# Spectral layer and two expert layers on one core: when constants are loaded, and how weight decoding is spread

## The chip, the core and the metric

The kernel runs on one core of a Trainium2 chip. Times are microseconds of device time for one execution; the kernel before has three of them and their median is what the prediction is compared with. The profile is of one further execution.

## The reference, cut to what matters

```python
X = np.fft.rfft(x, axis=1)                    # x: 2 x 3008 x 256, float32
Yr = Xr @ w_r - Xi @ w_i + b_r
Yi = Xr @ w_i + Xi @ w_r + b_i
Yr, Yi = shrink(Yr, 0.01), shrink(Yi, 0.01)   # soft threshold
y = np.fft.irfft(Y, n=3008, axis=1)
h = y @ w_in;   y = (h - tanh(h)) @ w_out                      # 256 x 2048, 2048 x 256
h = y @ w_in2;  out = (h * clip(h + 3, 0, 6) / 6) @ w_out2     # the same sizes
```

The four expert matrices arrive as float64.

## The kernel before, in words

**First stage: the spectral layer.** 3008 is split as 47 x 64. `dft_a` (16 calls, 8 per batch; L270) transforms along 47 with the matrix `amt`, two PSUM banks per call; ACT copies the banks back into the tile of x (L288) and stores it to DRAM, `s1` (L289). Batch 0 is done ahead of the main loop from eight tiles `xa`, batch 1 inside it from a ring of three tiles `xb`. The main loop (L664) has 24 iterations t, each on two of the 2 x 24 rows. `load_bi` reads `s1` back into a ring of three (`bi_all`, 512 KB for two iterations); a batch's first such load needs all eight of its stores. `dft_b(t+2)` (L310) transforms along 64 with the constants `bmt`; ACT evicts it as high part `fh` (L317, L318), DVE makes the low part `fl` (L324), ACT a negated copy (`evict_b_neg`, L329). `linear(t)` is 24 matmuls with the weights. `shrink(t)` is three DVE instructions (L351 to L353); then ACT makes `sh` and DVE `sl` (`shrink_split`, by L115 and L116). `dft_c(t-2)` transforms back along 64 with `cmH` and `cmL`; ACT evicts it (L377) and SP stores it to `s2`. Each pair of loads of `cmH` and `cmL` (2 x 256 KB, on POOL's queue, L623) serves two iterations. `dft_d` (L403) with `dmt` (35 KB) ends the transform and makes the operands of the second stage.

**Weight decoding.** The 32 blocks ("units") of the four matrices, 1i, 1o, 2i, 2o with 8 each, come as raw float64 words (512 KB a unit, `w_load`, on SP's queue, three buffers) and are made into two float32r parts by a generator, `w_steps`. The loops advance it step by step with `w_step`, so decoding is laid between other work by hand. A unit has seven steps (kind i, with four sums more) or five (kind o): two ACT instructions (L168, L169); two DVE tensor_scalars (L171, L172); the low part of the unit before (L203); a DVE instruction that frees the raw buffer and behind it the next `w_load` (L175); an addition (L179); for kind i four sums (L185 to L189); ACT's rounding to the high part (L197). `ptr["dec"]` counts finished units. In the first stage there are two steps before `shrink_split` and NST = 3 after it, from t = 0 until NDEC = 16 units are done, all of 1i and then all of 1o; the units of the second matrix pair follow in the second stage, and go back to DRAM.

**Second stage: the experts.** Sixteen super-groups k (0 to 7 the first expert, 8 to 15 the second) of eight groups g. A group (`group`, L568) is seven products into the banks al, be and ga in a scheme of sums (Strassen's), the nonlinearity, and the output matmuls of the group before into the four banks `acc`. Group (0,0) is written out as `first_group` at the end of the first stage. `super_hook` is called at five points (a to e) of a group; it lays the decode steps (three per group, at b, c and d: in all groups of k = 0, in groups 1 to 5 of k = 1 to 7) and the preparation of the next operands. `w_until` runs the generator on until a unit is done; it stands only at super-group 7 and after.

**What sets the order.** The kernel is written under a manual schedule: every engine and every DMA queue takes its instructions in program order, with the waits of their tiles. SP's queue carries x, raw, bmt, bi_all and the stores to s2; ACT's the stores to s1; POOL's the loads of cm. PSUM has eight banks: al (2), be, ga, and acc (4); `bank("h")` walks through al, be, al, ga.

Of the kernel before, what the change touches and what calls it, by code (L numbers as in the profile page):

```python
# [87 lines left out]
def spectral_moe_kernel(ctx: ExitStack, tc: tile.TileContext, x, w_r, w_i, b_r, b_i,  # L88
# [35 lines left out]
    wst = ctx.enter_context(tc.tile_pool(name="wst", bufs=2))  # L124
    dmt = perm.tile([96, 94], F32, name="dmt")
    three = perm.tile([128, 1], F32, name="three")
    wia = ctx.enter_context(tc.tile_pool(name="wia", bufs=1))
    wpool, W = {}, {}

# [4 lines left out]
        W[nm, c] = pl.tile([128, 2, n], F32R, tag=f"w{kind}{c}", name=f"w{kind}{c}")  # L134
        return W[nm, c]

    NDEC, NST = 16, 3
    w_src = {"1i": w1i, "1o": w1o, "2i": w2i, "2o": w2o}
    w_order = [(nm, c) for nm in ("1i", "1o", "2i", "2o") for c in range(8)]
    w_raw = {}  # L140
    ptr = {"load": 0, "dec": 0}

    def w_load(n=1):
        for _ in range(n):
            if ptr["load"] >= len(w_order):
# [12 lines left out]
    w_ws = {}  # L158

    def w_words(nm, c):  # L160
        u = w_raw.pop((nm, c)).bitcast(U32).rearrange("p (n two) -> p n two", two=2)
        lw, hw = u[:, :, 0], u[:, :, 1]
        ws = wst.tile([128, 8, 128], F32, tag="ws", name="ws")
        w_ws[nm, c] = ws
        taf = ws[:, 0:4, :].rearrange("p a f -> p (a f)")
        ta = taf.bitcast(U32)
        rnd = ws[:, 4:8, :].rearrange("p a f -> p (a f)").bitcast(U32)
        act.activation(out=taf, in_=hw.bitcast(F32), func=ACTF.Abs)  # L168
        act.activation(out=rnd, in_=lw, func=ACTF.Copy, scale=2.0 ** -29)  # L169
        yield  # L170
        dve.tensor_scalar(out=taf, in0=taf, scalar1=CLAMP, scalar2=None, op0=ALU.max)  # L171
        dve.tensor_scalar(out=ta, in0=ta, scalar1=3, scalar2=0x3FFFFFF8,  # L172
                          op0=ALU.logical_shift_left, op1=ALU.bitwise_and)
        yield "lo"
        dve.scalar_tensor_tensor(out=ta, in0=hw, scalar=0xC0000000, in1=ta,  # L175
                                 op0=ALU.bitwise_and, op1=ALU.bitwise_or)
        w_load()
        yield
        dve.tensor_tensor(out=ta, in0=ta, in1=rnd, op=ALU.add)  # L179

    def w_sums(nm, c):
        ws = w_ws[nm, c]
        if nm[1] == "i":
            yield
            dve.tensor_tensor(out=ws[:, 4, :], in0=ws[:, 0, :], in1=ws[:, 2, :], op=ALU.add)  # L185
            dve.tensor_tensor(out=ws[:, 6, :], in0=ws[:, 1, :], in1=ws[:, 0, :], op=ALU.subtract)
            yield
            dve.tensor_tensor(out=ws[:, 5, :], in0=ws[:, 4, :], in1=ws[:, 1, :], op=ALU.subtract)
            dve.tensor_tensor(out=ws[:, 7, :], in0=ws[:, 3, :], in1=ws[:, 5, :], op=ALU.subtract)  # L189
            src = ws[:, 1:8, :].rearrange("p a f -> p (a f)")  # L190
        else:
            src = ws[:, 0:4, :].rearrange("p a f -> p (a f)")
        if nm[0] == "1":
            t = alloc_w(nm, c)
        else:
            t = mo["w"].tile([128, 2, 896 if nm[1] == "i" else 512], F32R, tag="wout", name="wout")
        act.activation(out=t[:, 0, :], in_=src, func=ACTF.Copy)  # L197
        w_ws[nm, c] = (t, src)
        yield

    def w_lo(nm, c):
        t, src = w_ws.pop((nm, c))
        dve.tensor_tensor(out=t[:, 1, :], in0=src, in1=t.bitcast(F32)[:, 0, :], op=ALU.subtract)  # L203
        if nm[0] == "2":
            sp.dma_start(out=(w2id if nm[1] == "i" else w2od)[c], in_=t.bitcast(F32))

    def w_steps():
        for k, unit in enumerate(w_order):
            for step in w_words(*unit):
                yield  # L210
                if step == "lo" and k:
                    w_lo(*w_order[k - 1])
                    ptr["dec"] = k
                    yield
            yield from w_sums(*unit)
        w_lo(*w_order[-1])
        ptr["dec"] = len(w_order)

    w_gen = w_steps()

# [49 lines left out]
    def dft_a(i, finish=True):  # L270
        b, c = divmod(i, 8)
        xt = (x1[c % 3] if b else x0[c])[0:96]
        banks_ = []
        for g in range(2):
            p = bank("h")
            pv = p[0:96].rearrange("p (u d) -> p u d", d=D)
            for u in range(2):
                pe.matmul(out=pv[:, u, :], lhsT=amt, rhs=xt[:, 2 * g + u, :], start=True, stop=True)
            banks_.append(pv)
        if finish:  # L280
            dft_a_out(i, banks_)
        return banks_
# [71 lines left out]
        s = y  # L354
        s_t[j] = (s, sh, sl)

    def shrink_split(j, eng):
        s, sh, sl = s_t[j]
        split(sh, sl, s, eng)
        s_t[j] = (sh, sl)  # L360

    def dft_c(j):
# [250 lines left out]
    with tc.manual_schedule():  # L613
# [3 lines left out]
            if g < 6:  # L617
                sp.dma_start(out=bmt[:, 4 * g:4 * g + 4, :], in_=bv[:, 4 * g:4 * g + 4, :])

        def load_cm(g):  # L620
            if g < 6:
                for h, t in enumerate((cmH, cmL)):
                    pool.dma_start(out=t[:, 512 * g:512 * g + 512], in_=cm[:, h, 512 * g:512 * g + 512])  # L623

# [19 lines left out]
        load_bi(1)  # L644
        load_x(8)
        load_x(9)
        w_load()
# [16 lines left out]
        for t in range(NP):  # L664
            linear(t)
            if t > 1:
                dft_c(t - 2)
            if t + 2 < NP:
                dft_b(t + 2)
            ab = dft_a(a_next, False) if a_next < 16 else None  # L670
            if t > 1:
                evict_c(t - 2)
            if t + 2 < NP:
                evict_b_hi(t + 2)
            shrink(t)
            if t + 2 < NP:
                evict_b_lo(t + 2)
            if t == NP - 1:
                first = first_group()
                next(first)  # L680
            for _ in range(2):
                if ptr["dec"] < NDEC:
                    w_step()
            shrink_split(t, dve)
            for nm in {20: ("b11", "b21"), 21: ("t1",), 22: ("t2", "b22")}.get(t, ()):
                op_lo(0, nm)
            if t == 20:
                op_sub(T1, B12, B11, dve)
            if t == 21:
                op_sub(T2, B22, T1, dve)  # L690
            if t + 2 < NP:
                evict_b_neg(t + 2)
            if ab:
                dft_a_out(a_next, ab)
                a_next += 1
            flush_stores()
            if t % 2 == 0:
                load_bm(t // 2 + 2)
                load_cm(t // 2 + 1)
            if t > 0:  # L700
                load_x(10 + t)
            if t % 2 == 1:
                load_bi((t + 1) // 2 + 2)
            for _ in range(NST):
                if ptr["dec"] < NDEC:
                    w_step()
            if t == 9:
                sp.dma_start(out=dmt, in_=dm)
            if t == 14:
                load_din(0, din0)  # L710
            if t == 17:
                load_din(1, bi_ring[0])
            if t in (16, 17):
                dft_d(0, t - 16, "h")
            if t in (19, 20):
                dft_d(1, t - 19, "h")
            for nm in {19: ("b11", "b21"), 20: ("t1",), 21: ("t2", "b22")}.get(t, ()):
                op_hi(0, nm)
            if t == 22:
                op_sub(T3, B22, B12)  # L720
                op_sub(T4, B21, T2)
# [15 lines left out]
        def super_hook(k, g, pos):  # L737
# [92 lines left out]
```

## Time and profile before

| | us |
|---|---|
| median of 3 runs | 1255.49 (1254.61 to 1255.74) |
| the profiled execution | 1255.02 |
| its span, first to last instruction | 1253.2 |
| busy: PE, DVE, ACT, POOL | 1196.6, 974.3, 879.2, 165.0 |

The span and the execution's own time differ by what lies around the first and the last instruction. PE is TensorE, DVE VectorE, ACT ScalarE, POOL GpSimd, SP the engine that issues most of the DMAs. L12 is line 12 of the kernel. An instruction row has its start, its length, engine, line, operation, output and input; in brackets stand the idle time ahead of it on its engine and what ended it. The busy shares are means over stages that have different limits, so the rows further on are cut by stage.

### The profile page before, as it was taken

What the parts mean: (1) busy time and instruction counts of PE and PEld (TensorE: products, weight loads), DVE (VectorE), ACT (ScalarE), POOL (GpSimd) and SP (SyncE); (2) the same over time, 40 slices, a digit from 0 to 9 for tenths busy, and PEclk for the clock granted to TensorE, in tenths of its full rate; (3) what the DMA queues carried; (4) which work ended last, traced back from release to release, by engine and by line L of the source; (5) the groups of instructions that cost most, each with busy time, mean ns of one, the idle gap of its engine ahead of it and who ended that gap; (6) DMA issues with size and microseconds to landing.
All of it is one profiled execution on the core that took longest, in us unless ns stands there. A gap on an engine that the chain in (4) does not pass through costs nothing.

```text
span 1253.2 us, 20926 instructions
## 1 busy us (share of the span) xinstructions
PE 1196.6 (95%) x7824; PEld 1167.3 (93%) x7824; DVE 974.3 (78%) x1833; ACT 879.2 (70%) x1836; POOL 165.0 (13%) x165
## 2 busy tenths in 40 slices
PE   6788799989999999999999999999999999999998
PEld 4688698989999999999999999999999999999998
DVE  0487988788888888888868787878787878787775
ACT  3365666777777777777767677777777777777775
POOL 3000000220202020110202130202020202020200
PEclk8889999999999999999999999999999999999999
DMA  9874642131222222202001650000001010101000
GB/s 312 247 232 154 184 152 85 58 115 63 76 68 73 71 76 68 85 26 72 29 1 49 215 195 11 22 30 22 30 14 38 11 40 8 44 5 46 1 26 25
DMA packets 47797, 96.51 MB, mean 77 GB/s; under 512 B 4448, under 2 KB 27488, under 8 KB 47696
## 3 DMA queue, kind: packets, MB, share of 16 engines
q1 hardware_dynamic: 41728, 74.08, 18.8%
q0 software_dynamic: 4032, 14.68, 3.6%
q10 hardware_dynamic: 1936, 6.42, 1.5%
q8 instruction: 61, 1.00, 0.3%
q14 instruction: 40, 0.33, 0.1%
HBM read 58.73 MB, written 36.44 MB: 76 GB/s over the span
## 4 chain that ended last, share of the span: by engine, by line
PE 59%; DVE 17%; ACT 16%; issue 4%; DMA 3%; SPq 0%; ACTq 0%; DVEq 0%
PE acc L119 10%; PE acc L120 10%; PE acc L121 10%; PE al L119 5%; PE al L120 5%; PE al L121 5%; ACT gh L115 5%; DVE g L445 4%; DVE gl L116 3%; PE be L121 2%; PE be L120 2%; PE be L119 2%; ACT e L444 2%; DVE g L448 1%; PE ga L119 1%
## 5 line engine op out<-in xcount | busy, mean ns | idle before, releaser
L116 DVE TENSOR_TENSOR gl<-g,gh 128x376 fp32r<-128x376 f32 x502 | 286.4, 571 | 149.9 <-ACT gh L115 120.1
L115 ACT ACTIVATE gh<-g 128x376 fp32r<-128x376 f32 x509 | 263.9, 518 | 188.0 <-DVE g L445 92.6
L120 PE MATMUL acc<-wo,gh 128*128 128x256 f32 (+1 forms) x768 | 215.7, 281 | 0.0
L119 PE MATMUL acc<-wo,gh 128*128 128x256 f32 (+1 forms) x768 | 215.5, 281 | 0.0
L121 PE MATMUL acc<-wo,gl 128*128 128x256 f32 (+1 forms) x768 | 215.2, 280 | 0.0
L119 PE MATMUL acc<-gh,wo 128*128 128x376 f32 x512 | 173.2, 338 | 0.0
L121 PE MATMUL acc<-gh,wo 128*128 128x376 f32 x512 | 171.0, 334 | 0.0
L120 PE MATMUL acc<-gl,wo 128*128 128x376 f32 x512 | 171.0, 334 | 0.0
L412 POOL TENSOR_TENSOR bmt<-bmt 128x376 f32<-128x376 f32 x62 | 74.9, 1208 | 593.3 <-ACT bmt L405 449.3
L121 PEld LDWEIGHTS acc<-wo,gl 128*128 128x128 f32 (+1 forms) x768 | 143.0, 186 | 0.0
L120 PEld LDWEIGHTS acc<-wo,gh 128*128 128x128 f32 (+1 forms) x768 | 142.9, 186 | 0.0
L119 PEld LDWEIGHTS acc<-wo,gh 128*128 128x128 f32 (+1 forms) x768 | 142.7, 186 | 0.0
L448 DVE SCALAR_TENSOR_TENSOR g<-e,c 128x376 f32<-128x376 f32 x192 | 118.5, 617 | 12.6 <-ACT e L447 8.7
L445 DVE TENSOR_TENSOR g<-c,e 128x376 f32<-128x376 f32 x189 | 113.6, 601 | 14.0 <-ACT e L444 11.8
L447 ACT ACTIVATE e<-c,three 128x376 f32<-128x376 f32 x192 | 117.0, 609 | 7.7 <-DVE c L594 7.3
L428 POOL TENSOR_TENSOR cmL<-bmt,cmH 128x376 fp32r<-128x376 f32 x60 | 64.9, 1082 | 317.8 <-ACT cmH L423 317.8
L444 ACT ACTIVATE e<-c 128x376 f32<-128x376 f32 x189 | 97.8, 517 | 3.9 <-DVE c L594 3.7
L119 PE MATMUL al<-cmH,wi 128*128 128x376 f32 x256 | 88.6, 346 | 9.1 <-ACT s L580 7.4
L119 PEld LDWEIGHTS acc<-gh,wo 128*128 128x128 f32 x512 | 96.4, 188 | 0.0
L120 PEld LDWEIGHTS acc<-gl,wo 128*128 128x128 f32 x512 | 96.2, 188 | 0.0
L121 PEld LDWEIGHTS acc<-gh,wo 128*128 128x128 f32 x512 | 96.2, 188 | 0.0
L584 ACT ACTIVATE s<-be 128x376 f32<-128x376 f32 x127 | 61.9, 487 | 37.7 <-PE be L121 37.7
(164 smaller groups left out, 2870.9 us busy)
## 6 DMA issues: line engine op xcount, KB each, us to landing
raw<-in_moe_w_in_dram SPq DMA_DIRECT2D x16, 512.0 KB, 4.3
raw<-in_moe_w_out_dram SPq DMA_DIRECT2D x16, 512.0 KB, 4.2
w2id<-wout SPq DMA_DIRECT2D x8, 896.0 KB, 3.7
wi<-w2id POOLq DMA_DIRECT2D x8, 896.0 KB, 4.9
bi_all<-s SPq DMA_DIRECT2D x12, 512.0 KB, 4.4
y1d<-y SPq DMA_DIRECT2D x32, 188.0 KB, 2.5
bmt<-y1d SPq DMA_DIRECT2D x8, 752.0 KB, 5.2
s<-co SPq DMA_DIRECT2D x23, 256.0 KB, 2.9
```

The costliest lines, as they stand in the source:

```text
L115: act.activation(out=hi, in_=src, func=ACTF.Copy)
L116: (lo_eng or dve).tensor_tensor(out=lo, in0=src, in1=hi.bitcast(F32), op=ALU.subtract)
L119: pe.matmul(out=out_ap, lhsT=lh, rhs=rh, start=start, stop=False, **kw)
L120: pe.matmul(out=out_ap, lhsT=lh, rhs=rl, start=False, stop=False, **kw)
L121: pe.matmul(out=out_ap, lhsT=ll, rhs=rh, start=False, stop=stop, **kw)
L412: eng.tensor_tensor(out=out, in0=a, in1=b, op=ALU.subtract)
L428: (eng or dve).tensor_tensor(out=l, in0=OPS[nm][0], in1=h.bitcast(F32), op=ALU.subtract)
L444: act.activation(out=e, in_=src, func=ACTF.Tanh)
L445: dve.tensor_tensor(out=g, in0=src, in1=e, op=ALU.subtract)
L447: act.activation(out=e, in_=src, func=ACTF.Relu, bias=three)
L448: dve.scalar_tensor_tensor(out=g, in0=e, scalar=6.0, in1=src, op0=ALU.min, op1=ALU.mult)
L584: act.activation(out=s5, in_=be, func=ACTF.Copy)
```

## The change

Constants: `load_cm` gets a second argument; a one-element copy on POOL that reads it stands ahead of each pair of cm loads. The first pair reads the last tile of batch 0's `dft_a`, the others `sh` of the iteration that issues them. `dmt` is loaded at the start instead of at t = 9; `load_x(8)` stands ahead of `load_bi(0)`, `load_x(9)` ahead of `load_bi(1)`. Of the three raw loads ahead of the loop one is left; the other two come at t = 0 and t = 1.

Decoding: units of 1i and 1o alternate; 13 instead of 16 are done in the first stage, with four steps per iteration instead of five and none at t = 0 and 1. ACT's rounding of a unit is issued one step into the next unit, behind that unit's tensor_scalars, and its low part two steps later. In super-group 0 a fourth step is laid at point a, and `w_until` stands ahead of every group.

Loop order: `sh` is issued straight behind `shrink`, and `evict_b_neg` ahead of the first decode steps.

PSUM: in batch 0's `dft_a`, every second call takes two banks of `acc`.

```diff
-    NDEC, NST = 16, 3
+    NDEC, NST = 13, 2
-    w_order = [(nm, c) for nm in ("1i", "1o", "2i", "2o") for c in range(8)]
+    w_order = [(nm, c) for c in range(8) for nm in ("1i", "1o")]
+    w_order += [(nm, c) for nm in ("2i", "2o") for c in range(8)]
...
+    def w_steps():
+        prev = None
+        for k, (nm, c) in enumerate(w_order + [(None, 0)]):
+            if nm:
...
+                act.activation(out=taf, in_=hw.bitcast(F32), func=ACTF.Abs)
+                act.activation(out=rnd, in_=lw, func=ACTF.Copy, scale=2.0 ** -29)
+                yield
+                dve.tensor_scalar(out=taf, in0=taf, scalar1=CLAMP, scalar2=None, op0=ALU.max)
+                dve.tensor_scalar(out=ta, in0=ta, scalar1=3, scalar2=0x3FFFFFF8,
+                                  op0=ALU.logical_shift_left, op1=ALU.bitwise_and)
+            if prev:
...
+                act.activation(out=t[:, 0, :], in_=src, func=ACTF.Copy)
+                yield
+            if nm:
+                dve.scalar_tensor_tensor(out=ta, in0=hw, scalar=0xC0000000, in1=ta,
+                                         op0=ALU.bitwise_and, op1=ALU.bitwise_or)
+                w_load()
+                yield
+            if prev:
+                dve.tensor_tensor(out=t[:, 1, :], in0=src, in1=t.bitcast(F32)[:, 0, :], op=ALU.subtract)
...
+                ptr["dec"] = k
+                yield
...
+            dve.tensor_tensor(out=ta, in0=ta, in1=rnd, op=ALU.add)
             yield
...
-            p = bank("h")
+            p = bank("acc" if i < 8 and i % 2 else "h")
...
-        def load_cm(g):
+        def load_cm(g, after):
             if g < 6:
+                pool.tensor_copy(out=gate[0:1, 0:1], in_=after)
                 for h, t in enumerate((cmH, cmL)):
...
+        sp.dma_start(out=dmt, in_=dm)
...
-        w_load()
         for i in range(8):
             dft_a(i)
+        load_x(8)
         load_bi(0)
+        load_x(9)
         load_bi(1)
-        load_x(8)
-        load_x(9)
-        w_load()
         load_bm(1)
-        load_cm(0)
+        load_cm(0, x0[7][0:1, 3, 0:1])
         load_x(10)
         w_load()
...
             shrink(t)
+            shrink_hi(t)
             if t + 2 < NP:
                 evict_b_lo(t + 2)
...
+            if t + 2 < NP:
+                evict_b_neg(t + 2)
             for _ in range(2):
-                if ptr["dec"] < NDEC:
+                if t > 1 and ptr["dec"] < NDEC:
                     w_step()
-            shrink_split(t, dve)
+            shrink_lo(t)
...
-                load_cm(t // 2 + 1)
+                load_cm(t // 2 + 1, s_t[t][0].bitcast(F32)[0:1, 0, 0:1])
             if t > 0:
                 load_x(10 + t)
+            if t in (0, 1):
+                w_load()
...
-                if pos in "bcd" and k < NS:
+                if (pos in "bcd" or k == 0 and pos == "a") and k < NS:
                     w_step()
...
+                if k == 0:
+                    w_until(2 * g + 2)
                 group(k, g, prev, lambda pos: super_hook(k, g, pos))
```

## Rows read from the trace of the kernel before

**Rows 1.** The page's slices: DMA busy in tenths, 40 slices of 31.3 us.

```profile
DMA  9874642131222222202001650000001010101000
```

**Rows 2.** Windows: stretch, length; busy of PE, PEld, DVE, ACT, POOL; clock, DMA share, GB/s.

```profile
34.60:46.18 11.58, 6.71 (x41) 6.56 (x41) 2.18 (x4) 2.47 (x6) 0.00 (x0) 0.67 0.92 258
34.60:104.02 69.42, 61.36 (x427) 57.19 (x428) 47.99 (x94) 40.11 (x80) 0.00 (x0) 0.90 0.78 231
46.18:76.41 30.23, 30.23 (x225) 28.24 (x225) 24.00 (x48) 19.02 (x38) 0.00 (x0) 1.00 0.72 210
104.02:177.92 73.90, 58.73 (x435) 55.98 (x434) 63.85 (x117) 41.72 (x84) 0.00 (x0) 0.93 0.53 165
177.92:196.86 18.94, 18.93 (x155) 18.58 (x155) 17.41 (x31) 14.47 (x30) 2.28 (x2) 1.00 0.26 87
206.00:268.81 62.81, 60.14 (x354) 58.40 (x353) 50.38 (x98) 45.39 (x96) 16.87 (x15) 1.00 0.22 72
268.81:610.88 342.07, 334.42 (x1965) 326.30 (x1964) 287.57 (x550) 252.62 (x543) 45.72 (x41) 1.00 0.21 70
610.88:676.88 66.00, 65.88 (x394) 65.35 (x393) 50.17 (x94) 47.18 (x102) 8.83 (x8) 1.00 0.04 13
```

**Rows 3.** Timeline of the start: banks of dft_a on PE, first loads of bi_all.

```profile
11.99 1.03 PE L278 MATMUL al<-xa,amt 96*96 96x256 f32 x4
...
12.86 1.03 PE L278 MATMUL be<-xa,amt 96*96 96x256 f32 x4
...
20.92 1.12 PE L278 MATMUL al<-xa,amt 96*96 96x256 f32 x4 [1.85 <-ACT xa L288]
...
34.62 0.92 SPq L299 DMA_DIRECT2D bi_all<-s  x2
```

**Rows 4.** Timeline of PE: dft_b of iterations 0 and 5.

```profile
46.18 1.13 PE L310 MATMUL al<-bmt,bi_all 128*128 128x128 f32 x8 [0.87 <-DMA bmt<-in_bm_dram]
...
76.41 1.05 PE L310 MATMUL be<-bmt,bi_all 128*128 128x128 f32 x8
```

**Rows 5.** Timeline of DVE: L351 of iterations 0, 15, 16; last decode instruction of the stage.

```profile
45.35 0.69 DVE L351 TENSOR_TENSOR ly<-acc,bias 128x512 f32<-128x512 f32 x1 [1.12 <-PE acc L121]
...
145.49 0.69 DVE L351 TENSOR_TENSOR ly<-acc,bias 128x512 f32<-128x512 f32 x1
...
151.69 0.68 DVE L351 TENSOR_TENSOR ly<-acc,bias 128x512 f32<-128x512 f32 x1
...
182.20 0.69 DVE L203 TENSOR_TENSOR wo<-ws,wo 128x512 fp32r<-128x512 f32 x1
```

**Rows 6.** Waits, 104.02 to 177.92 us: total, times, longest.

```profile
ACT wo L197 <- DVE ws L179: 17.1, 7, 2.8
```

**Rows 7.** Timeline of ACT and PE in super-group 0, near 259 us.

```profile
258.32 0.95 ACT L197 ACTIVATE wout<-ws 128x896 fp32r<-128x896 f32 x1 [1.94 <-DVE ws L189]
...
260.47 0.44 PE L119 MATMUL al<-cmH,wi 128*128 128x376 f32 x1 [1.70 <-ACT s L580]
```

**Rows 8.** DMA queues from 0 to 34.6 us: POOL's; share of the 16 engines.

```profile
q0 software_dynamic: 1728, 3.15, 29.3%
```

**Rows 9.** DMA issues, whole run: queue, count, KB each, median us to landing.

```profile
wi<-w2id POOLq DMA_DIRECT2D x8, 896.0 KB, 4.9
...
s<-xb ACTq DMA_DIRECT2D x8, 384.0 KB, 4.4
```

**Rows 10.** Instruction groups of DVE by shape, 104 to 178 us: busy, mean ns.

```profile
L175 DVE SCALAR_TENSOR_TENSOR ws<-raw,ws 128x512 uint32<-128x512 uint32 x10 | 6.9, 686 | 0.0
...
L352 DVE TENSOR_SCALAR lc<-ly 128x512 f32<-128x512 f32 x11 | 4.7, 427 | 0.4
...
L203 DVE TENSOR_TENSOR wi<-ws,wi 128x896 fp32r<-128x896 f32 x3 | 3.3, 1085 | 0.0
...
L189 DVE TENSOR_TENSOR ws<-ws 128x128 f32<-128x128 f32 x3 | 0.9, 292 | 0.1
```

**Rows 11.** Tile cmH, up to 60 us: its loads, issue to landing.

```profile
DMA to landing us min/median/max: 9.2/15.8/17.9
```

More of the change, by code (lines that the diff above doesn't have):

```diff
@@ L126, in spectral_moe_kernel @@
     three = perm.tile([128, 1], F32, name="three")
+    gate = perm.tile([1, 1], F32, name="gate")
     wia = ctx.enter_context(tc.tile_pool(name="wia", bufs=1))
@@ L158, in spectral_moe_kernel @@
     w_ws = {}
[L160 to L176, printed above, removed]
-        w_load()
-        yield
-        dve.tensor_tensor(out=ta, in0=ta, in1=rnd, op=ALU.add)
@@ L181, in w_sums @@
-    def w_sums(nm, c):
-        ws = w_ws[nm, c]
-        if nm[1] == "i":
-            yield
[L185 to L209, printed above, removed]
-                yield
[L211 to L217, printed above, removed]
+    def w_steps():
+        prev = None
+        for k, (nm, c) in enumerate(w_order + [(None, 0)]):
+            if nm:
+                u = w_raw.pop((nm, c)).bitcast(U32).rearrange("p (n two) -> p n two", two=2)
+                lw, hw = u[:, :, 0], u[:, :, 1]
+                ws = wst.tile([128, 8, 128], F32, tag="ws", name="ws")
+                taf = ws[:, 0:4, :].rearrange("p a f -> p (a f)")
+                ta = taf.bitcast(U32)
+                rnd = ws[:, 4:8, :].rearrange("p a f -> p (a f)").bitcast(U32)
+                act.activation(out=taf, in_=hw.bitcast(F32), func=ACTF.Abs)
[5 more added lines that the diff above has]
+            if prev:
+                pn, pc, src = prev
+                if pn[0] == "1":
+                    t = alloc_w(pn, pc)
+                else:
+                    t = mo["w"].tile([128, 2, 896 if pn[1] == "i" else 512], F32R, tag="wout", name="wout")
+                act.activation(out=t[:, 0, :], in_=src, func=ACTF.Copy)
[7 more added lines that the diff above has]
+                dve.tensor_tensor(out=t[:, 1, :], in0=src, in1=t.bitcast(F32)[:, 0, :], op=ALU.subtract)
+                if pn[0] == "2":
+                    sp.dma_start(out=(w2id if pn[1] == "i" else w2od)[pc], in_=t.bitcast(F32))
+                ptr["dec"] = k
+                yield
+            if not nm:
+                return
+            dve.tensor_tensor(out=ta, in0=ta, in1=rnd, op=ALU.add)
+            yield
+            src = taf
+            if nm[1] == "i":
+                dve.tensor_tensor(out=ws[:, 4, :], in0=ws[:, 0, :], in1=ws[:, 2, :], op=ALU.add)
+                dve.tensor_tensor(out=ws[:, 6, :], in0=ws[:, 1, :], in1=ws[:, 0, :], op=ALU.subtract)
+                yield
+                dve.tensor_tensor(out=ws[:, 5, :], in0=ws[:, 4, :], in1=ws[:, 1, :], op=ALU.subtract)
+                dve.tensor_tensor(out=ws[:, 7, :], in0=ws[:, 3, :], in1=ws[:, 5, :], op=ALU.subtract)
+                src = ws[:, 1:8, :].rearrange("p a f -> p (a f)")
+                yield
+            prev = (nm, c, src)
@@ L355, in shrink, with shrink_hi, shrink_lo @@
         s_t[j] = (s, sh, sl)
-    def shrink_split(j, eng):
+    def shrink_hi(j):
         s, sh, sl = s_t[j]
-        split(sh, sl, s, eng)
+        act.activation(out=sh, in_=s, func=ACTF.Copy)
+    def shrink_lo(j):
+        s, sh, sl = s_t[j]
+        dve.tensor_tensor(out=sl, in0=s, in1=sh.bitcast(F32), op=ALU.subtract)
         s_t[j] = (sh, sl)
@@ L639, in spectral_moe_kernel @@
                          in_=w.rearrange("(o d) -> o d", o=1).broadcast_to([64, D]))
-        w_load()
         for i in range(8):
             dft_a(i)
+        load_x(8)
         load_bi(0)
+        load_x(9)
         load_bi(1)
-        load_x(8)
-        load_x(9)
-        w_load()
         load_bm(1)
-        load_cm(0)
+        load_cm(0, x0[7][0:1, 3, 0:1])
         load_x(10)
@@ L690, in spectral_moe_kernel @@
                 op_sub(T2, B22, T1, dve)
-            if t + 2 < NP:
-                evict_b_neg(t + 2)
             if ab:
@@ L704, in spectral_moe_kernel @@
             for _ in range(NST):
-                if ptr["dec"] < NDEC:
+                if t > 1 and ptr["dec"] < NDEC:
                     w_step()
-            if t == 9:
-                sp.dma_start(out=dmt, in_=dm)
             if t == 14:
```

## The prediction, made before the changed kernel was run

> **What bounds the kernel now.** I read the page's slices first: in tenths of their time the DMA engines are at 9 until 31 us, at 8 and 7 until 94, at 4 to 6 until 188, then mostly at 2 or less [rows 1]. So the start is a matter of transfers. Next I cut the span with the view of windows, at the starts of named instructions: L351 (DVE's first instruction on an iteration t of the first stage) for t = 8, 19 and 23, L580 (ACT's first on a group of the second stage) for groups (0,1), (1,0), (6,0) and (7,0) [rows 2]. Four limits stand one behind the other:
>
> - *Until 34.6 us*: the transforms of batch 0 must all be stored before SP can issue the first load of bi_all at 34.62 [rows 3]. PE, ACT and DVE wait for that.
> - *Iterations 0 to 5*: PE is busy for 30.23 of 30.23 us, five iterations of 6.05 us; the stretch from 34.6 to 104.0 as a whole has the DMA engines busy for 0.78 of it [rows 2, 4].
> - *Iterations 8 to 19*: DVE is busy for 63.85 of 73.90 us, PE only 58.73 [rows 2]; the iteration between the two rows of [rows 5] at 145.49 and 151.69 takes 6.20 us. ACT waits 17.1 us for DVE's last decode step (L179) before it can round (L197) [rows 6].
> - *Second stage*: PE, almost. From (0,1) it idles 62.81 - 60.14 = 2.67 us; in super-groups 1 to 5, which carry decode steps, 342.07 - 334.42 = 7.65 us; super-group 6, without any, takes 66.00 us with PE busy for 65.88 [rows 2]. The idle time has a form: ACT stands 1.94 us at L197 for DVE, and PE's next product 1.70 us for ACT's L580 behind it [rows 7].
>
> **The start.** Twelve loads of cm ran at once on POOL's queue: 29.3% of the 16 engines over 34.6 us, 10.1 us of transfer time [rows 8]. All but the first pair now come later, and so does the first raw block (512 KB, as much as two cm loads: 1.7 us); the first xb load (376 KB) moves in front of bi_all, and dmt (35 KB) is small. If transfers were all that bounds, bi_all would be issued some 9 to 10 us earlier. But PE needs its time: one bank of dft_a takes 0.87 us (11.99 to 12.86 [rows 3]); sixteen banks, of which four are done at 11.99, end at 11.99 + 12 x 0.86 = 22.3, then 0.6 us for the last eviction, 0.3 for the issue, 4.4 for the store to land (that of the later stores [rows 9]): 27.6 us instead of 34.6. The eight banks take away the wait of PE for ACT (1.85 us at 20.92 [rows 3]) and are part of this; alone they would bring little, since ACT itself waited for stores there. **-7.0 us** at bi_all, bounds -3 (ACT held by its stores again) and -10.
>
> **Iterations 0 to 8.** What was removed from the start is now moved here. Transfer time from 34.6 to 104.0 was 0.78 x 69.4 = 54.1 us. Added: ten cm loads, 8.4 us; less the xb load that went ahead, 1.2 (376 KB at that price); of raw there are seven blocks as before (one ahead of the loop, one each in iterations 0 and 1, then one per unit). That makes 61.3 us. The highest share that the trace shows for a stretch with this mix is 0.92, from 34.6 to 46.2 [rows 2]; at that, 66.6 us, iteration 8 begins at 27.6 + 66.6 = 94.2 instead of 104.0: **-9.8 us so far** (the 7.0 included). The bounds: PE at 6.05 us per iteration begins iteration 8 at 45.35 - 7.0 + 48.4 = 86.8, -17 (45.35 is L351 of iteration 0 [rows 5]); at the old share of 0.78, 78.6 us, at 106.2, +2. I take 0.92, because of what is moved only half is urgent: cm is wanted over three iterations after its issue, raw two units later. Decode no longer stands in iterations 0 and 1; PE has no gain from that, but SP's queue has: a raw load waits there for DVE's L175, with xb and bi_all loads behind it.
>
> The gate on POOL waits for sh of the same iteration, and behind it stand only the two cm loads; nothing else is POOL's before iteration 20. It costs nothing that anything waits for.
>
> **Iterations 8 to 19.** DVE's own work on an iteration is four instructions of 0.69 us (L351 [rows 5] and its like) and one of 0.43 (L352): 3.19. A unit of kind i has two of 0.43, two of 0.69, four of 0.29 and the low part of 1.09, 4.48; one of kind o two of 0.43 and three of 0.69, 2.93 [rows 10]. Before, an iteration with one o unit: 3.19 + 2.93 = 6.12, measured 6.20 [rows 5], so I add 0.1 to such a sum. After: four steps per iteration, with twelve steps to a pair (7 of i, 5 of o), 7.41 / 3 = 2.47; 3.19 + 2.47 + 0.1 = 5.76. Eleven iterations: 63.3 instead of 73.9, **-10.6 us**. PE's floor lies lower there, as dft_a has ended. ACT's rounding no longer waits for the sums of its own step, and sh and neg stand ahead of the decode steps on ACT; so I price what the new order adds at nothing, DVE covering it. If the two engines still wait in turn, 6.2 remains: -5.7. If no bubble remains: -11.7.
>
> **Iterations 19 to 23.** Sixteen units took 100 steps at five per iteration, gone by iteration 19. Thirteen take 81 at four, from iteration 2 on: to the middle of 22. So three iterations and one step, 3 x 2.47 + 0.6 = 8.0 us of DVE, come to where 1.5 stood (unit 15's last instructions, the one at 182.20 [rows 5] and two of 0.43), beside op_lo and op_sub. DVE has 18.94 - 17.41 = 1.53 us of idle there [rows 2]; I give it 1.0. **+5.5 us** (bounds +4 and +6.5).
>
> **Second stage.** 192 - 81 = 111 steps are left instead of 92. Super-group 0 takes 28 instead of 21: 7 x 0.62 = 4.3 us more of DVE where it idles 62.81 - 50.38 = 12.4 [rows 2]; I put 1.5 of it on the path and take the 2.67 of PE's idle time away: **-1.2** (bounds -2.7 and +4.3). The w_until ahead of each group finds its units done (13 at the start, four steps per group, 14 needed at group 6, 16 at group 7). Super-groups 1 to 5 took 342.07 - 5 x 66.00 = 12.1 us more than 6 for 71 steps, 0.17 each. Rounding a step later I let take away half of PE's 7.65 us, 3.9; twelve more steps, into super-group 6, cost 2.0: **-2** (bounds -6 and +2).
>
> **Sum.** -9.8 - 10.6 + 5.5 - 1.2 - 2.0 = -18.1 us. The profiled execution took 1255.0 (span 1253.2 and 1.8 around it): 1236.9. The median of the runs is 0.5 above it: **1237**.
>
> **Rivals.**
> - *Transfers keep up*: iteration 8 begins near 87 and the rest goes as above or a little better: 1237 - 7 = 1230. For: much of the moved load has time. Against: 61.3 us of transfers would have to fit into 86.8 - 27.6 = 59.2. Chance 0.26.
> - *Transfers do not pack tighter* than 0.78, or ACT and DVE still wait in turn: +2.2 instead of -9.8 gives 1249; 6.2 us per iteration gives 1242. For: even before, with a good fifth of their time free, the DMA engines were the last to be ready at 46.18 [rows 4]. Chance 0.20 together, 0.03 of it within 0.2% (2.5 us, about what a measurement here can tell from no change).
> - *Slower, by cm coming late*: dft_c of iteration t + 4 needs the pair issued at t; the lead is over three iterations, 17 us. If a pair lands after L us, each of five pairs costs L - 17; from L = 21.1 on, 5 x 4.1 = 20.6 us eat the gain of 18.1 and the 2.5 that a measurement can tell, and the run is slower. For: at the start, with full queues, cm landed after 9.2 to 17.9 us [rows 11]. Against: POOL-queue loads of 896 KB in super-group 7, beside a busy DVE, landed in 4.9 us [rows 9]. At 22 us the time is 1237 + 25 = 1262. Chance 0.04. [...]
>
> The forecast has 0.50. **Range**: 1226 (transfers keep up, and most of the second stage's better bounds: -6 there instead of -2) to 1250 (the old share). What lies outside is the cm rival and the ends of the bounds where several fall together, some 0.15. Faster 0.93, same 0.03, slower 0.04.
>
> **What would show it.** In the trace after: bi_all issued near 27.6; iteration 8 near 94 with a DMA share near 0.9 from there; iterations of about 5.8 us until 22; iteration 23 near 182 instead of 196.9; no ACT wait at the rounding; PE idle under 1 us in super-group 0. Wrong, if bi_all is issued after 31, if PE waits for xb, bi_all or cm by over 10 us in all, or if super-group 0 grows by over 4.

## The result, and the profile after

| | before | after |
|---|---|---|
| median, us (four runs each, side by side) | 1255.62 | **1224.92** |
| lowest to highest | 1254.61 to 1257.50 | 1222.61 to 1227.01 |
| the profiled execution (span) | 1255.02 (1253.2) | 1225.3 (1223.5) |

The ratio of the two is 0.9753 (95%: 0.9732 to 0.9775): 30.7 us less. Forecast were 18 less, 1237, and the result lies 1.1 us below the stated range. Cut at the same instructions as [rows 2] and by the two profiled executions, in us:

| stage | before | after | difference | forecast |
|---|---|---|---|---|
| start of iteration 0 | 45.35 | 42.61 | -2.7 | -7.0 |
| iterations 0 to 8 | 58.67 | 49.04 | -9.6 | -2.8 |
| iterations 8 to 19 | 73.90 | 58.31 | -15.6 | -10.6 |
| iterations 19 to 23 | 18.94 | 24.75 | +5.8 | +5.5 |
| iteration 23 to group (0,1) | 9.14 | 11.11 | +2.0 | 0 |
| group (0,1) to (1,0) | 62.81 | 63.30 | +0.5 | -1.2 |
| (1,0) to the last output of the first expert | 476.34 | 465.73 | -10.6 | -2.0 |
| from there to the end of the execution | 509.87 | 510.45 | +0.6 | 0 |

The page's slices after, 40 of 30.6 us each:

```profile
DMA  9896622222212132211104540101010101000000
```

Against [rows 1], the third slice stands at 9 instead of 7 and the fourth at 6 instead of 4: transfers have moved from the start into iterations 0 to 8, and they run there at a higher share (0.92 in the window below, 0.78 in that of [rows 2] from 34.60). The windows of the stages in the table (columns as in [rows 2]; the first is the stretch before iteration 0, the last two are super-groups 1 to 5 and 6):

```profile
31.90:42.61 10.71, 6.74 (x42) 6.71 (x43) 1.39 (x3) 2.47 (x6) 0.00 (x0) 0.65 1.02 272
42.61:91.65 49.04, 48.74 (x361) 45.25 (x360) 38.25 (x70) 34.45 (x68) 5.20 (x12) 1.00 0.92 294
91.65:149.96 58.31, 54.54 (x445) 53.62 (x443) 56.57 (x108) 40.47 (x80) 1.23 (x3) 0.97 0.61 191
149.96:174.71 24.75, 21.26 (x169) 20.25 (x167) 23.49 (x42) 15.37 (x31) 2.43 (x2) 1.00 0.38 110
174.71:185.82 11.11, 7.42 (x32) 6.68 (x31) 7.21 (x15) 6.57 (x15) 1.00 (x1) 0.69 0.14 47
185.82:249.12 63.30, 59.73 (x345) 57.38 (x345) 55.45 (x105) 47.74 (x101) 17.96 (x15) 0.99 0.26 77
249.12:580.53 331.41, 330.91 (x1967) 328.33 (x1966) 286.47 (x554) 253.58 (x543) 44.84 (x41) 1.00 0.21 71
580.53:646.53 66.00, 65.88 (x394) 65.26 (x393) 53.57 (x101) 48.90 (x106) 8.83 (x8) 1.00 0.08 29
```

Three things are to be seen. Iterations 0 to 8 are PE's: 48.74 of 49.04 us busy. In iterations 8 to 19 DVE is busy for 56.57 of 58.31, where it was 63.85 of 73.90. And super-groups 1 to 5, with their decode steps, leave PE 0.50 us idle in 331.41 (7.65 before): they take 66.28 us each, where super-group 6 takes 66.00.

The rounding is where the form of the work differs. It costs most in the iterations on units of kind i. Iteration 8 of the kernel before, DVE, ACT and PE:

```profile
106.72 0.29 DVE L189 TENSOR_TENSOR ws<-ws 128x128 f32<-128x128 f32 x1
107.05 0.95 ACT L197 ACTIVATE wi<-ws 128x896 fp32r<-128x896 f32 x1 [3.89 <-DVE ws L189]
...
109.00 0.61 ACT L115 ACTIVATE sh<-ly 128x512 fp32r<-128x512 f32 x1
109.52 0.40 ACT L329 ACTIVATE fl<-fl 128x256 fp32r<-128x256 f32 x1
109.65 0.69 DVE L116 TENSOR_TENSOR sl<-ly,sh 128x512 fp32r<-128x512 f32 x1 [2.63 <-ACT sh L115]
...
109.97 0.39 PE L121 MATMUL acc<-lwH,fl 128*128 128x256 f32 x1 [2.69 <-ACT fl L329]
```

ACT stands 3.89 us until DVE has made the unit's last sum. `sh` and the negated copy stand behind the rounding on ACT and come later (`sh` starts at 109.00, though DVE had ended its operand at 105.89); then DVE stands 2.63 us for `sh` and PE 2.69 us for the copy. Each engine waits in turn, and the iteration takes 8.64 us. With a unit of kind o, in the iteration of [rows 5], ACT stands too, but DVE hardly does:

```profile
145.61 0.63 ACT L197 ACTIVATE wo<-ws 128x512 fp32r<-128x512 f32 x1 [2.38 <-DVE ws L179]
...
147.52 0.69 DVE L324 TENSOR_TENSOR fl<-al,fh 128x512 fp32r<-128x512 f32 x1 [0.15 <-ACT fh L318]
```

The 6.20 us of this iteration are DVE's own work. An iteration of the kernel after, where the rounding is L184, the eviction of dft_b L310 and `sh` L352:

```profile
122.95 0.62 ACT L184 ACTIVATE wo<-ws 128x512 fp32r<-128x512 f32 x1
...
123.63 0.68 DVE L344 TENSOR_TENSOR ly<-acc,bias 128x512 f32<-128x512 f32 x1
123.96 0.57 ACT L310 ACTIVATE fh<-al 128x512 fp32r<-128x512 f32 x1
...
124.35 0.43 DVE L345 TENSOR_SCALAR lc<-ly 128x512 f32<-128x512 f32 x1
...
125.54 0.63 ACT L352 ACTIVATE sh<-ly 128x512 fp32r<-128x512 f32 x1 [0.74 <-DVE ly L346]
...
128.96 0.68 DVE L344 TENSOR_TENSOR ly<-acc,bias 128x512 f32<-128x512 f32 x1
```

The rounding takes operands that were ready a step ago, waits for nothing, and ACT goes on to the evictions. The period is 5.33 us (123.63 to 128.96), with four decode steps in it where the one above has five. With the late rounding alone and five steps (the third experiment), iterations 8 to 11 take 4.98 us less than before, and the seven iterations behind them only 1.29 less.

The waits of 104.02 to 177.92 us before (total, times, longest): the rounding of kind i, which comes on top of [rows 6], and PE's wait for what ACT makes out of `fl`:

```profile
ACT wi L197 <- DVE ws L189: 9.3, 3, 3.9
...
PE acc L121 <- ACT fl L329: 4.9, 5, 2.7
```

and of 91.65 to 149.96 after, which has no row for the rounding or for ACT's `fl` among PE's:

```profile
ACT sh L352 <- DVE ly L346: 10.8, 9, 3.1
...
PE acc L121 <- DVE fl L317: 1.3, 3, 0.6
```

ACT now waits mostly in front of `sh`. With `sh` at its old place the time is the same (see the experiments).

In iterations 0 to 8 the delay of DVE also reaches PE through SP's queue. The next raw load stands there until DVE has freed a buffer, and a load of xb stands behind it. SP's wait between 64 and 76 us before, PE's stop for that load, and the window behind the stop:

```profile
SPq L154 <- DVE ws L175: 7.9, 1, 7.9
```

```profile
80.64 1.99 PE L278 MATMUL al<-xb,amt 96*96 96x256 f32 x4 [3.18 <-DMA xb<-in_x_dram]
```

```profile
80.64:88.85 8.21, 8.21 (x39) 7.12 (x39) 4.90 (x12) 4.49 (x10) 0.00 (x0) 0.63 0.95 295
```

PE stops for 3.18 us, and over the next 8.21 us the granted clock is 0.63, where it was 1.00 from 46.18 to 76.41 [rows 2]; the products with the weights start 0.21 us apart there until 86.5 and 0.12 from 86.8 on. So the dft_b at 88.85 comes 12.4 us after the one at 76.41, where the five before are at most 6.2 apart: 6.3 us of this stage lie at one place. With the late rounding alone PE's longest wait for xb in this stage is 0.25 us.

At the start, the timeline of ACT after:

```profile
19.33 0.31 ACTq L282 DMA_DIRECT2D s<-xa  x1
19.74 0.59 ACT L281 ACTIVATE xa<-al 96x512 f32<-96x512 f32 x1 [3.28 <-DMA lwf<-in_w_i_dram]
```

that of POOL:

```profile
25.44 0.17 POOL L619 COPY gate<-xa 1x1 f32<-1x1 f32 x1 [21.97 <-ACT xa L281]
```

and that of SP:

```profile
29.18 0.40 SPq L292 DMA_DIRECT2D bi_all<-s  x1
```

The load of bi_all is issued 5.4 us earlier than in [rows 3], but ACT stood 3.28 us in front of a store, and iteration 0 begins 13.4 us after the issue where it was 10.7. The first pair of cm, xb and bmt run beside bi_all now (DMA share 1.02); that they cause this is not shown.

### The profile page after: what moved, and what is told of

It is laid out like the page before. It is cut to its first block, busy times and chain, and to the rows that moved or that the text cites. A ratio compares the mean times of both kernels' runs of the same rounds, so it can differ in the third digit from the quotient of the medians.

```text
span 1223.5 us, 20909 instructions
## 1 busy us (share of the span) xinstructions
PE 1184.0 (97%) x7824; PEld 1163.9 (95%) x7824; DVE 972.6 (79%) x1833; ACT 880.4 (72%) x1836; POOL 166.0 (14%) x171
## 4 chain that ended last, share of the span: by engine, by line
PE 77%; DVE 9%; ACT 8%; issue 3%; DMA 2%; SPq 0%; ACTq 0%; DVEq 0%
PE acc L119 13%; PE acc L121 13%; PE acc L120 13%; PE al L119 7%; PE al L120 6%; PE al L121 6%; PE be L121 3%; PE be L120 3%; PE be L119 3%; ACT gh L115 2%; PE ga L400 2%; DVE g L442 2%; PE ga L120 2%; PE ga L121 2%; PE ga L119 2%
```

## The experiments

The questions: is the late rounding (theory R) or the thinner spread of the decode steps (rival S) what pays, and what do the single parts bring? Ratios are to the kernel before, with 95% intervals.

**The rounding back in its own unit, all else as after.**

```diff
-            if prev:
-                pn, pc, src = prev
...
-                act.activation(out=t[:, 0, :], in_=src, func=ACTF.Copy)
                 yield
...
-            prev = (nm, c, src)
...
+            act.activation(out=t[:, 0, :], in_=src, func=ACTF.Copy)
+            yield
+            prev = (nm, c, src, t)
```

> The changed kernel with one thing undone: ACT's rounding of a unit stands again at the end of that unit, behind its own sums, with the same number of steps, the same order of units and the same spread. Theory R (the rounding's wait on ACT is what cost the second stage its idle time on PE, and part of iterations 8 to 19): super-groups 1 to 5 go from 331.4 us back to about 340, iterations 8 to 19 from 58.3 to 61 or more, together 1237 to 1241. Rival S (the gain comes from the thinner spread, four steps instead of five and units of both kinds in turn): both stretches stay within 2 us, 1225 to 1229.

1261.46, ratio 1.0046 (1.0028 to 1.0063): without this one move the changed kernel is slower than the one before, and 20 us slower than R expected. The waits from the start of super-group 1 on, 269.6 to 613 us:

```profile
PE al L119 <- ACT s L577: 7.3, 6, 2.5
...
ACT wout L208 <- DMA w2od<-wout: 7.0, 2, 3.9
...
ACT wout L208 <- DVE ws L202: 4.8, 5, 1.3
```

The rounding (here L208) waits for DVE again, and PE for `s` behind it. But 7.0 us are a wait for a store of decoded weights, which the kernel before does not have: this variant still has the low part, and the store behind it, one step later. So a cleaner one was wanted.

**Exactly the old order of the decode steps, all else as after.** Beside the edit above, the instruction that frees raw stands behind the low part again.

```diff
-            if nm:
-                dve.scalar_tensor_tensor(out=ta, in0=hw, scalar=0xC0000000, in1=ta,
-                                         op0=ALU.bitwise_and, op1=ALU.bitwise_or)
-                w_load()
-                yield
             if prev:
                 dve.tensor_tensor(out=t[:, 1, :], in0=src, in1=t.bitcast(F32)[:, 0, :], op=ALU.subtract)
...
                 yield
+            if nm:
+                dve.scalar_tensor_tensor(out=ta, in0=hw, scalar=0xC0000000, in1=ta,
+                                         op0=ALU.bitwise_and, op1=ALU.bitwise_or)
+                w_load()
+                yield
```

> The changed kernel with the steps of a unit in exactly the old order: rounding at the unit's end and the low part of the unit before ahead of the instruction that frees the raw buffer. In the first experiment the low part stood one step later, and ACT then also waited 7.0 us for the store of wout; without that wait theory R expects 1250 to 1256, that is, with the old order of steps everything else in the change is worth 0 to 6 us. Rival (the rest of the change is worth what the stages suggest, 10 us and more): 1246 or less.

1260.36, ratio 1.0038 (1.0024 to 1.0051), again above R's range. The store's wait is gone and the time is the same. Its super-group 0, windows and then waits:

```profile
199.75:272.22 72.47, 64.17 (x356) 61.78 (x355) 59.22 (x106) 47.88 (x100) 16.41 (x15) 0.95 0.24 75
```

```profile
PE al L119 <- DVE c L598: 4.2, 3, 2.8
...
ACT wo L208 <- DVE ws L194: 3.2, 2, 1.6
```

With the old order, 28 steps instead of 21 make this super-group 72.47 us; with the late rounding it is 63.30.

**Only the new order of the decode steps, put into the kernel before.** Its generator is replaced by that of the change; `NDEC`, `NST` and `w_order` stay.

```diff
-    def w_words(nm, c):
...
-    def w_sums(nm, c):
...
-    def w_lo(nm, c):
...
     def w_steps():
+        prev = None
+        for k, (nm, c) in enumerate(w_order + [(None, 0)]):
...
```

> The kernel before with only the new generator: rounding one step into the next unit; 16 units in the first stage, five steps per iteration, the old order of units, loads and loop as before. Theory R: super-groups 1 to 5 go from 342.1 us to 332, and iterations 8 to 19 from 73.9 to 69 or less, so 1241 to 1246. Rival S: 1253 to 1256.

1228.86, ratio 0.9782 (0.9768 to 0.9797): nearly the whole gain from one edit, and far more than R expected of it. Windows of its iterations 0 to 8 and 8 to 19, its super-group 0, and super-groups 1 to 5:

```profile
44.74:95.43 50.69, 49.57 (x365) 46.08 (x366) 46.81 (x94) 36.69 (x72) 0.00 (x0) 1.00 0.82 253
95.43:163.06 67.63, 57.55 (x445) 55.52 (x444) 62.36 (x114) 43.71 (x88) 0.00 (x0) 0.95 0.60 183
191.65:253.00 61.35, 59.10 (x354) 58.54 (x353) 52.13 (x98) 45.34 (x96) 16.52 (x15) 1.00 0.19 65
253.00:584.70 331.70, 330.66 (x1965) 327.21 (x1964) 285.01 (x549) 253.04 (x543) 45.95 (x41) 1.00 0.22 72
```

Against before: -8.0, -6.3, -1.5 and, from 342.07, -10.4. All four stages gain, super-groups 1 to 5 nearly as much as in after (331.41); iterations 8 to 19 stay DVE's, as five steps per iteration are still laid there. In iterations 0 to 8 DVE's waits for ACT fall from 10.6 us to 2.4.

The two orders with the two surroundings make a table (medians, us):

| | old order of decode | late rounding |
|---|---|---|
| all else as before | 1255.6 | 1228.9 |
| all else as after | 1260.4 | 1224.9 |

Late rounding is worth 27 us with the old surroundings and 35 with the new. Everything else together costs 5 without it and brings 4 with it, which the intervals do not quite separate. The new order also has the low part and the freeing of raw at other places. With the new surroundings these were tried apart: the first experiment has both where after has them, so it differs from after in the rounding alone, and it is no faster than the second. With the old surroundings they were not.

**The gates taken away, all else as after.**

```diff
-                pool.tensor_copy(out=gate[0:1, 0:1], in_=after)
```

> The changed kernel without the one-element copies on POOL, so that the twelve loads of cm run at once; all else stays. Theory T (iterations 0 to 8 are bound by PE with or without these transfers, so the gates are worth only what bi_all is delayed): iteration 0 begins 3 to 5 us later, iterations 0 to 8 stay at 49 us, 1228 to 1231. Rival 1 (the gates are worth the whole transfer time of ten loads): 1233 or more. Rival 2 (the stores of batch 0 are held by something else and the gates are worth nothing): 1224 to 1226.

1230.67, ratio 0.9800 (0.9784 to 0.9817): the gates are worth 5.7 us, as T expected. Of these 4.4 lie ahead of iteration 0, which begins at 46.98 instead of 42.61 when all cm loads start at once; bi_all is issued at 35.78 instead of 29.18. Its iterations 0 to 8:

```profile
46.98:96.37 49.39, 48.77 (x361) 45.24 (x360) 38.23 (x70) 34.39 (x68) 0.00 (x0) 1.00 0.79 252
```

49.39 us at a DMA share of 0.79, 49.04 at 0.92 with the gates: transfers do not set the pace of this stage in either.

**The old spread of the decode steps and order of the units, all else as after.**

```diff
-    NDEC, NST = 13, 2
+    NDEC, NST = 16, 3
...
-                if t > 1 and ptr["dec"] < NDEC:
+                if ptr["dec"] < NDEC:
...
-                if (pos in "bcd" or k == 0 and pos == "a") and k < NS:
+                if pos in "bcd" and k < NS:
```

> The changed kernel with the old spread: 16 units in the first stage, five steps per iteration from iteration 0 on, all of 1i before 1o, three steps per group in super-group 0; late rounding, gates, loads and loop order stay. Theory M (three units were only moved: what iterations 8 to 19 gained, the end of the stage and super-group 0 gave back): 1223 to 1228, with iterations 8 to 19 near 67, 19 to 23 near 19.5, the stretch up to (0,1) 9.1 and super-group 0 near 61.4. Rival (the spread is worth what iterations 8 to 19 show, 9 us): 1232 or more.

1230.57, ratio 0.9797 (0.9784 to 0.9810): the thin spread is worth 5.6 us, more than M allows and less than its rival, and at another place. Iterations 8 to 19 take 67.41 instead of 58.31, but 19 to 23 only 19.34 instead of 24.75, and super-group 0 61.32 instead of 63.30; with 0.5 at the end of the first stage, 7.9 of the 9.1 us come back. What is left is in iterations 0 to 8:

```profile
39.85:95.68 55.83, 52.68 (x365) 48.31 (x364) 47.03 (x94) 37.04 (x72) 5.19 (x12) 0.94 0.84 269
```

55.83 us, with PE idle for 3.15. Five steps in the kernel before with the late rounding (50.69, above) are not so slow, nor are four steps with the gates (49.04). Five steps with the gates and the units alternating take 52.16 (the early steps below). That the gates are what disturbs five steps is not shown: the kernel with 50.69 differs in the other loads as well.

**The eight banks undone.**

```diff
-            p = bank("acc" if i < 8 and i % 2 else "h")
+            p = bank("h")
```

> The changed kernel with the four old banks in batch 0's dft_a. If PE's wait for a free bank bounds the start, bi_all comes 2 to 4 us later and the time is 1227 to 1229. Rival: ACT, whose stores wait, sets the pace whatever the banks: 1224.5 to 1226.

1225.13, ratio 0.9753 (0.9738 to 0.9767): worth nothing; bi_all is issued at 29.19 against 29.18.

**`sh` and `neg` at their old places.**

```diff
             shrink(t)
-            shrink_hi(t)
...
-            if t + 2 < NP:
-                evict_b_neg(t + 2)
             for _ in range(2):
...
+            shrink_hi(t)
             shrink_lo(t)
...
+            if t + 2 < NP:
+                evict_b_neg(t + 2)
```

> The changed kernel with sh and the negated copy back behind the first two decode steps, as before. If ACT's order in the loop matters by itself, PE waits for the negated copy or dft_c for sl, and iterations 8 to 23 lengthen by 4 us or more: 1229 or more. If late rounding already took the blocking away: 1224 to 1227.

1223.85, ratio 0.9744 (0.9731 to 0.9758): worth nothing either. One place differs: at the end of the first stage it takes 9.51 us where after takes 11.11. The row that it does not have, from after's waits between 174.71 and 185.82 us:

```profile
PE al L119 <- ACT bi_all L540: 3.0, 1, 3.0
```

In iteration 23 `sh` stands ahead of the first group's evictions on ACT and makes it wait 3.26 us for DVE. It is given back elsewhere (super-group 0 takes 0.8 more).

**Prologue: the loads of `lwf` behind batch 0's dft_a, the first cm pair behind the landing of bi_all.**

```diff
-        lws = []
-        for w in (w_r, w_i):
...
             dft_a(i)
+        lws = []
+        for w in (w_r, w_i):
...
-        load_cm(0, x0[7][0:1, 3, 0:1])
+        load_cm(0, bi_ring[0][0:1, 0, 0:1])
```

> The changed kernel with the two loads of lwf issued behind batch 0's dft_a instead of ahead of it, and the first pair of cm gated by the landing of the first bi_all instead of by the last tile of x. Theory Q (one store of batch 0 waits on ACT 3.3 us for a load of lwf issued eight DMAs before it, and the first bi_all lands late because cm runs beside it): bi_all is issued 2 to 4 us earlier, lands 1 to 2 us sooner after its issue, 1219 to 1222. Rival (PE's pace and the transfers of x and s set it): 1224 to 1226.

1223.75, ratio 0.9742 (0.9728 to 0.9755): slower than Q's range and just below its rival's. ACT's stop for `lwf` is 0.44 us instead of 3.28; ahead of the store where the 3.28 stood it stands 0.95 for a load of x, and 1.75 for PE at the next. bi_all is issued at 27.70, iteration 0 begins at 39.42 instead of 42.61, and of the 3.2 us the total shows 1.2, which the intervals do not separate from nothing. In single executions of the seven kernels that share after's prologue bi_all is issued between 27.99 and 29.66, and iteration 0 begins between 39.85 and 42.61, with a median of 40.89. So differences of a us or two there say little, and after's own profile is the latest of the seven to begin. This variant and the last one below begin at 39.42 and 38.72.

**Five steps per iteration while PE is the bound (t under 8), from t = 0.**

```diff
-                if t > 1 and ptr["dec"] < NDEC:
+                if ptr["dec"] < NDEC:
...
-            for _ in range(NST):
+            for _ in range(NST + (t < 8)):
```

> The changed kernel with five decode steps per iteration in iterations 0 to 7, four after that, still 13 units. Iterations 0 to 8 are bound by PE with DVE idle for 10.8 of 49.0 us, so by theory P the work moved there is hidden and iterations 19 to 23 come back to about 19.5 and the stretch behind them to 9.1: 1217 to 1221. Rival (the earlier raw loads and the fuller ACT stretch iterations 0 to 8 by as much): 1224 to 1227.

1222.98, ratio 0.9735 (0.9721 to 0.9748). Iterations 19 to 23 fall from 24.75 to 20.15, the end of the stage from 11.11 to 10.23, but 0 to 8 rise from 49.04 to 52.16 (the six kernels with four steps there and the late rounding take 49.04 to 50.06). The time lies between the two forecasts, and the gain over after is within the intervals.

**No decode steps in groups 6 and 7 of super-group 0.**

```diff
-            if 1 <= g < 6 or k == 0 and g > 0:
+            if 1 <= g < 6:
```

> The changed kernel with no decode steps in groups 6 and 7 of super-group 0, where POOL works on the next operands: the eight steps go to later super-groups. Theory C (DVE's instructions stretch beside POOL's there, the low part of a unit from 1.09 to 1.89 us, one sum from 0.28 to 1.09, and PE waits 2.6 us for DVE behind them): super-group 0 goes from 63.3 to 60 or 61, later ones stay at 66.0 to 66.8, 1222 to 1223. Rival (the steps cost the same wherever they stand): 1224.5 to 1226.

1221.38, ratio 0.9721 (0.9708 to 0.9735). What it removes is to be seen in the timeline of after, around group (0,7):

```profile
236.69 1.89 DVE L192 TENSOR_TENSOR wout<-ws,wout 128x896 fp32r<-128x896 f32 x1
237.59 1.85 POOL L116 TENSOR_TENSOR gl<-g,gh 128x376 fp32r<-128x376 f32 x1
...
240.53 1.03 POOL L425 TENSOR_TENSOR cmL<-bmt,cmH 128x376 fp32r<-128x376 f32 x1 [1.09 <-ACT cmH L420]
240.62 1.49 DVE L199 CUSTOM_DVE_ANT_0 ws<-ws 128x1024 uint16<-128x1024 uint16 x1
...
243.30 1.09 DVE L203 TENSOR_TENSOR ws<-ws 128x128 f32<-128x128 f32 x1
...
246.35 0.44 PE L119 MATMUL al<-t4h,wi 128*128 128x376 f32 x1 [2.64 <-DVE c L598]
```

POOL prepares the next operands here, and the three decode instructions of DVE shown take 0.8 us longer beside it than elsewhere (last section); PE then waits 2.64 us for DVE. The window of super-group 0 without those steps:

```profile
187.34:246.61 59.27, 58.94 (x351) 57.75 (x350) 50.05 (x96) 44.94 (x96) 16.66 (x15) 1.00 0.20 58
```

59.27 us instead of 63.30, PE idle for 0.33. Five kernels with after's super-group 0 show 63.30 or 63.31, so these 4.0 us are clear, though the intervals of the totals just touch. The eight steps cost nothing where they went: super-groups 1 to 5 take 331.10 us, 331.41 in after. That the rival is wrong is shown by this; that POOL is the reason rests on the lengths in the timeline.

**The last three together.** The edits are those of the prologue, of the early steps and of groups 6 and 7.

> The changed kernel with the later loads of lwf and the later gate of the first cm pair, five decode steps in iterations 0 to 7, and no decode steps in groups 6 and 7 of super-group 0. If the three gains add up (1.2, 1.9 and some 2.5 us): 1218.5 to 1220.5. Rival (the earlier start meets fuller queues in iterations 0 to 8, and two of them give the same time): 1221 to 1223.

**1215.76**, ratio 0.9678 (0.9665 to 0.9691): faster than both kernels and than either forecast, 9.2 us below after, with the intervals apart. Super-group 0 takes 59.25 us; its iterations 0 to 8 and 19 to 23:

```profile
38.72:90.88 52.16, 49.52 (x365) 45.68 (x364) 46.44 (x88) 38.12 (x75) 5.49 (x12) 1.00 0.95 298
149.54:169.49 19.95, 19.82 (x168) 19.66 (x168) 16.01 (x28) 12.41 (x25) 2.09 (x2) 1.00 0.20 68
```

Here the DMA engines stand at 0.95 in iterations 0 to 8.

## Why the prediction was right and wrong

The sign was right, and the time was missed by 12.1 us, because the part that makes most of the gain was priced at 3.9. By the table, three stages gained 20.4 us more than forecast and the others 8.9 less, so the miss would have been larger without errors the other way. **The failed step** is the price of the late rounding: "Rounding a step later I let take away half of PE's 7.65 us, 3.9", and in the first stage "I price what the new order adds at nothing, DVE covering it". Alone it brings 27. The rows were there: ACT's 17.1 us at L197 [rows 6], with 9.3 more for kind i that were not looked at, and the pair of 1.94 and 1.70 us [rows 7]. They were read as a delay on ACT that DVE's work covers. With units of kind o that is so: DVE stood 0.15 us in the iteration that was read. With units of kind i it is not: DVE's last sum, ACT's rounding, `sh` and the copy behind it, DVE and PE on those close a ring, and DVE stood 2.63 us in iteration 8 and PE 2.69.

- *Start, -7.0:* -2.7 at iteration 0 (up to -5.5 in the variants with the same prologue). At bi_all it is -5.4, within the bounds: issued at 29.18, not 27.6, with ACT held 3.28 us in front of a store, as the lower bound had it. The other miss is that the 10.7 us from there to iteration 0 were taken as they were. They became 13.4, and 11.1 to 13.3 in the six other executions with this prologue; without the gates they are 11.2, so the first cm pair is not shown to be the reason.
- *Iterations 0 to 8, "I take 0.92":* the share measured 0.92, and yet transfers were not the limit: PE was, at 6.13 us per iteration, and without gates it is as fast at 0.79. The rival "transfers keep up" was nearest, for a reason it did not give, though iteration 8 begins at 91.65 and not near 87. Late rounding alone brings 8.0 of the 9.6 us. The prediction named the raw load on SP's queue with xb behind it, but put no price on it; PE's stop for xb and the clock of 0.63 behind it were 6.3 us. That nothing waits behind POOL's gate held: the cm loads in the loop landed after 5.4 and 5.7 us (medians).
- *Iterations 8 to 19, -10.6:* -15.6, right in direction. The 5.76 us per iteration were 5.30 (58.31 / 11). Late rounding alone takes the stage from 73.90 to 67.63, everything else without it to 67.80, and both to 58.31. That the 6.20 us of the o iteration are DVE's work was right; what was mis-sized is the sum of recorded lengths with 0.1 on top. After's iteration of 5.33 us holds 5.81 of them, because they overlap (last section).
- *Iterations 19 to 23, +5.5:* +5.8, and undone by the old spread, so the cause is shown.
- *Iteration 23 to (0,1):* not priced, +2.0; 1.6 of it is `sh` ahead of the first group on ACT, as its return there shows.
- *Super-group 0, -1.2:* +0.5. "PE idle under 1 us" did not come: 3.57. The four steps per group are paid in groups 6 and 7, beside POOL: without them there the super-group takes 59.27 us, not 63.30.
- *Second stage, -2:* -10.6, the late rounding. The sum took half of PE's 7.65 us; of its own 12.1 us by which super-groups 1 to 5 exceed five of super-group 6, 10.7 went. The 100 steps of sixteen units are 98 by the generator, which moves no term by more than 0.4 us.
- *Slower, by cm coming late:* not seen: none of PE's waits in the trace of after is for cm. With DVE busy for 38.25 of 49.04 us, the loads in the loop landed after 5.4 and 5.7 us (medians) and after 8.5 at most, far from the 17 at which, by the prediction's estimate, they would delay anything.

What stays open: why five steps per iteration lengthen iterations 0 to 8 in the kernels with the gates; why ACT stops ahead of that store; and whether the last three edits, 6.6 us by their single medians, bring more together (9.2): the intervals do not tell.

## What to carry to other kernels

When an engine that keeps to program order, as ACT did in iteration 8 (3.89 us at one instruction, `sh` behind it), issues an instruction on what its neighbour has only just begun, price not its wait but everything queued behind it and who needs that, and look at the iteration in which the neighbour stands as well, not at one in which it is busy throughout. A step of slack at that one place was worth 27 us of 1256, more than all rearranged loads. Judge a moved load by the stage's window without it, not by the DMA share: 0.92 and 0.79 gave 49.04 and 49.39 us. Thinning work out in one stage pays only if the stage that takes it over has room: of 9.1 us, 7.9 came back.

## What the runs showed of the hardware that was not expected

**DVE's recorded lengths overlap.** From the iteration of after shown above, DVE alone:

```profile
125.42 0.69 DVE L317 TENSOR_TENSOR fl<-al,fh 128x512 fp32r<-128x512 f32 x1
126.02 0.68 DVE L187 SCALAR_TENSOR_TENSOR ws<-raw,ws 128x512 uint32<-128x512 uint32 x1
126.62 0.69 DVE L192 TENSOR_TENSOR wo<-ws,wo 128x512 fp32r<-128x512 f32 x1
127.22 0.69 DVE L356 TENSOR_TENSOR sl<-ly,sh 128x512 fp32r<-128x512 f32 x1
```

None of these reads what the one before it writes, and instructions of 0.69 us start 0.60 apart, so a sum of lengths overstates a row of them by up to 0.09 each. Where the next one does read it, as L345 reads what L344 writes, no overlap is recorded: L344 of 0.68 us and L345 start 0.72 apart (123.63 and 124.35), and in all 19 such pairs between 42 and 150 us the second starts 0.03 to 0.04 behind the end of the first.

**DVE beside POOL.** Around group (0,7) an instruction of 128 x 128 took 1.09 us instead of 0.28 to 0.29, the low part of 896 columns 1.89 instead of 1.09, the addition 1.49 instead of 0.69: 0.8 us longer for each of these, though a `gl` of 128 x 376 there took 0.89 instead of 0.55. Each of the three started 0.1 to 0.6 us behind one of POOL's (at 243.30, 236.69 and 240.62 behind 242.94, 236.08 and 240.53). The decode instruction L187 of 128 x 512, begun at 236.09 beside POOL's of 236.08, kept its 0.69. What made the three longer is not shown. Leaving these steps out of the two groups was worth 4.0 us of the super-group.

**ACT's stop ahead of one store.** In after, ACT's idle time of 3.28 us around the store at 19.33 us is put down to the landing of `lwf`, a load on SP's queue whose data the store does not touch. A stop of 3.2 to 3.9 us stands at this place in all seven kernels with this prologue and in the one with the old banks, but the view names `lwf` in five of the eight and PE or another store in the others. With the loads of `lwf` issued later it was 0.95 there. What ACT waited for is not shown.
